# Two expert blocks computed during the first search, rows of x written during attention, the last scatter after the branch

## Chip, core and metric

The kernel runs on one core of a Trainium2 chip. The time is the device time of one execution in microseconds (us), the median of the runs. The engines are PE (matmul), DVE (vector), ACT (scalar), POOL (GpSimd) and SP (issues DMAs). Each takes its own instructions in order.

## What is computed

Two stages. First an RWKV-5 attention over r, k, v of shape (4 batches, 8 heads, 768 steps, 48), in which a state per head decays by w at every step. Then the result, as 3072 rows (tokens) of 384, goes through a mixture of 8 experts that is balanced by a global greedy rule:

```python
cap = N // E                                   # 384
logits = x @ w_gate                            # (3072, 8)
for idx in np.argsort(-logits.flatten()):      # best (token, expert) pair first
    tok, e = idx // E, idx % E
    if assigned[tok] >= 0 or counts[e] >= cap:
        continue
    assigned[tok] = e
    counts[e] += 1
for e in range(E):
    h = np.maximum(x[assigned == e] @ w1[e], 0.0)   # 384 -> 1024
    out[assigned == e] = h @ w2[e]                  # 1024 -> 384
```

So every expert gets exactly 384 tokens, which is three blocks of 128.

## The kernel before

**Attention** (class `Mild`). The sequence is cut into 6 chunks of 128 steps. A unit is one batch's chunk; there are N = 24 units, ordered chunk by chunk, so units 0 to 3 are chunk 0 of the four batches and units 20 to 23 are chunk 5. `Mild.run` writes the order of the instructions out by hand, one round for each unit n. A round works on several units at once: `turn(n+2)` transposes keys and queries on PE (kT_ps L456, rT_ps L462) which ACT and DVE move out, `diagonal(n+2)` is eight ACT operations (L484), `pairs(n+1)` is eight matmuls into g_ps (L494) and two masked copies on DVE (L496), `outputs(n)` is y_ps (L530) with `keep(n)` between its halves (kv_ps L509). After every fourth unit `gate` (lg_ps L557) and `logits` (lt_ps L567) put the gate's logits into the table LG, [128, 24, 8].

**Rows of x.** Attention's result is held transposed. `rows` transposes a unit back (four PE transposes, x_ps L579), ACT copies it (xr L581) and SP writes it to a table in DRAM, `x_rows` (L585), from which experts gather their tokens. Units 0 to 3 are done in the last two rounds, the others between the steps of the first search.

**The search** (class `Assignment`). The greedy rule is replaced by filling events: `likely` looks for the largest threshold at which some expert has at least 384 tokens that prefer it. Each of three rounds (`count`) compares all tokens with 16 candidates on DVE (ind), sums on PE (counts L882, L894) and picks a digit on DVE. That gives the expert (`fmax`), its tokens (`acc`), and their places (st_ps L998, L999). `tokens` makes a list of 384 token numbers (row, oh, vals on DVE, some_ps L1138, list_ps L1148). `leave` takes the tokens and the expert out of LG. Seven events are searched; the eighth expert takes what is left (`remainder`). A flag `ok` says whether every event was as the search supposes.

**The first search** stands between attention and the experts. Its steps are written out by hand too (`tc.manual_schedule`), with `rows` in the hooks `walk.between`, and with matmuls that nobody reads (`idle`, L412, 12 and 28 of them). The first expert's weights are loaded a quarter early, the rest behind the gather.

**Experts** (class `Experts`). For each: three gathers on POOL (xg L1222), weights of 3 MB on SP (L1218), nine transposes (xT_ps L1238), 24 matmuls of 384 columns into h_ps (L1247) with ReLU on ACT (L1248), and 24 into o_ps (L1254), eight for each block of 128 tokens, whose result ACT copies (o_sb L1256) and POOL scatters to the output (L1257). One matmul in float32 leaves two records in the trace, one transpose one record. Buffers are double: `turns[n % 2]`. `run` fetches expert n+1 while n is computed; here the scheduler puts the next search's instructions between the matmuls.

**The branch.** At the end every engine loads `ok` (L905) and branches (L1303) past an arm that computes everything again in a general way, in case the flag is 0.

Of the kernel before, what the change touches and what calls it, by code (L numbers as in the profile page):

```python
# [26 lines left out]
def attention_any(ctx, tc, r, k, v, w, u, wg, x_dram, LG, ident, walk):  # L27
# [181 lines left out]
    def outputs(n):  # L209
# [21 lines left out]
        nc.scalar.dma_start(x_dram[ts(b * C + c, 128), :], xt)  # L231
# [17 lines left out]
    def gate(n):  # L249
# [12 lines left out]
        nc.scalar.copy(LG[:, i, :], lg_ps)  # L262
# [12 lines left out]
class Mild:  # L275
# [243 lines left out]
    def outputs(self, n):  # L519
# [25 lines left out]
        xT = self.xpool.tile([128, HP, T], F32, name=f"x{n}")  # L545
# [18 lines left out]
    def logits(self, c):  # L564
        nc, B, lg = self.nc, self.B, self.lg
        lt_ps = self.walk.ps.tile([128, T], F32, name="lt_ps", tag="few")
        nc.tensor.transpose(lt_ps, lg, self.ident)  # L567
        nc.scalar.copy(self.LG.rearrange("p (b c) e -> p b c e", b=B)[:, :, c, :],
                       lt_ps.rearrange("p (b e) -> p b e", b=B)[:, :, 0:self.E])

    def rows(self, ns, tag):
# [3 lines left out]
        ps = self.ps.tile(shape, F32, name="x_ps", tag=tag)  # L575
        P = PD + D
        for i, n in enumerate(ns):
            for o in range(HP):
                nc.tensor.transpose(ps[:, i, o, 0:P], self.xts[n][0:P, o, :], self.ident[0:P, 0:P])  # L579
        xr = self.pool.tile([128, 2, H, D], F32, name="xr", bufs=4)  # L580
        nc.scalar.copy(xr[:, 0:m].rearrange("p i h d -> p (i h) d"),  # L581
                       ps.rearrange("p i o (z d) -> p (i o z) d", z=2)[:, :, 0:D])
        for i, n in enumerate(ns):
            b, c = self.units[n]
            nc.sync.dma_start(self.x_dram[ts(b * C + c, 128), :], xr[:, i].rearrange("p h d -> p (h d)"))  # L585
# [10 lines left out]
    def run(self):  # L596
# [21 lines left out]
        for n in range(N):  # L618
# [10 lines left out]
            else:  # L629
                if n + 3 < N:  # L630
                    self.again(n + 3)
                if n + 2 < N:
                    self.own_sum(n + 2)
                    self.turn(n + 2)
                    self.diagonal(n + 2)
                if n <= B:
                    self.keep(n - 1)
                if n + 1 < N:
                    self.pairs(n + 1)
            if n + 3 < N:  # L640
# [7 lines left out]
            if n == N - 2:  # L648
                walk.guess(walk.ps.tile([128, 128], F32, name="most_ps", tag="few"), self.ident)
            if n >= N - 2:  # L650
                self.rows((2 * (n - N + 2),), "kT_ps")
                self.rows((2 * (n - N + 2) + 1,), "rT_ps")
# [3 lines left out]
            if n == N - 3:  # L656
                walk.guess_most(self.LG.rearrange("p (b c) e -> p b c e", b=B)[:, :, 0:C - 1, :], AX.XYZ)
# [10 lines left out]
        self.rows((4, 5), "g_ps")  # L668
        self.left = [(n, n + 1) for n in range(6, N, 2)]
        self.turns = 1  # L670

    def some_rows(self, m):
        for _ in range(m):
            if self.left:
                self.rows(self.left.pop(0), ("g_ps", "y_ps")[self.turns % 2])
                self.turns += 1


class Assignment:
# [21 lines left out]
    def __init__(self, ctx, tc, ML, CAP):  # L701
        self.tc, self.nc, self.ML, self.CAP = tc, tc.nc, ML, CAP
# [40 lines left out]
        new("ok", [128, 1], I32)  # L743

        self.outs = ctx.enter_context(tc.tile_pool(name="s_outs", bufs=2))
# [4 lines left out]
    def constants(self):  # L750
# [86 lines left out]
        yield  # L837
        nc.gpsimd.memset(self.last, float(E * (E - 1) // 2))
# [33 lines left out]
    def count(self, pool, m, prop, cand, digit_of):  # L872
# [3 lines left out]
        ind = pool.tile([128, NT, ND], BF16, name="ind")  # L876
# [4 lines left out]
        for j in range(NT // G):  # L881
# [12 lines left out]
        nc.tensor.matmul(all_ps.rearrange("p d e -> p (d e)"), self.ones_h,  # L894
                         wide.rearrange("p d e -> p (d e)"), start=True, stop=True)
# [12 lines left out]
    def fill(self):  # L908
# [3 lines left out]
        tok = self.tokens(out["place"])  # L912
        self.leave(out["fmax"], out["acc"])
        return out["fmax"], tok

    def general_fill(self):
# [6 lines left out]
        self.leave(out["fmax"], out["acc"])  # L923
        return out["fmax"], tok

# [4 lines left out]
    def leave(self, fmax, acc):  # L930

        nc, pool, tt = self.nc, self.pool, self.tt
        NT, E = self.NT, self.E
        fe = pool.tile([128, E], F32, name="fe")
# [8 lines left out]
    def likely(self, fmax, acc, place, on_fmax=None):  # L943
# [11 lines left out]
        for g in range(3):  # L955
            all_ps = self.count(pool, m, prop, cand, self.digit_of)
            if g == 0:
                eq = pool.tile([128, NT, E], F32, name="eq")
# [36 lines left out]
        if on_fmax is not None:  # L995
# [3 lines left out]
        nc.tensor.matmul(st_ps[:, 1, :], self.rest_of, acc, start=True, stop=True)  # L999

# [8 lines left out]
        flag = pool.tile([128, 1], I32, name="flag")  # L1009
        nc.vector.scalar_tensor_tensor(out=flag, in0=upto[:, NT - 1:NT], scalar=float(CAP), in1=n_sole,  # L1010
                                       op0=ALU.is_equal, op1=ALU.mult)
        tt(self.ok, self.ok, flag, ALU.mult)
        tt(upto, upto, st_ps[:, 1, :], ALU.add)
        nc.vector.scalar_tensor_tensor(out=place, in0=upto, scalar=128.0, in1=acc, op0=ALU.add, op1=ALU.mult)

    def surely(self, pool, fmax, acc, place):
# [6 lines left out]
        eq = pool.tile([128, NT, E], F32, name="eq")  # L1023
# [64 lines left out]
    def remainder(self):  # L1088
# [12 lines left out]
        return fmax, self.tokens(place)  # L1101
# [19 lines left out]
    def tokens(self, place, tok=None):  # L1121

        nc, pool, ps, NT, tt, LO = self.nc, self.pool, self.ps, self.NT, self.tt, self.LO
        NC, Q = self.CAP // 128, 128 // LO
# [4 lines left out]
        row = pool.tile([128, NT, LO], F16, name="row")  # L1129
        tt(row, self.by_token(lo, LO), self.by_expert(self.iota[:, 0:LO]), ALU.is_equal)  # L1130
        oh = pool.tile([128, NT, NC * Q], F16, name="oh")
        tt(oh, self.by_token(hi, NC * Q), self.by_expert(self.hi_of), ALU.is_equal)
# [208 lines left out]
```

## Time and profile before

| | |
|---|---|
| median of 3 runs | 424.08 us (423.92 to 424.22) |
| profiled execution | 423.93 us, its span 422.2 us |
| busy share | PE 94%, PEld 63%, DVE 42%, ACT 36%, POOL 32% |
| chain that ended last | PE 70%, issue 13%, DVE 5%, POOL 4%, DMA 3% |
| groups | h_ps 133.5 us in 384 records, o_ps 127.5 us in 384 records |
| DMA | 54.09 MB, mean 128 GB/s |

The span runs from the first to the last instruction of the execution; what lies outside it is the difference to its own time. PE's busy time is modelled, so a PE that is always busy need not be at its peak. "issue" is time in which the engine waited for nothing that the profile shows. The stages in time: attention until about 122 us, the first search and the first gather until about 153 us, the experts until about 412 us, the end until 422.2 us.

### The profile page before, as it was taken

How to read it: one execution, taken by the hardware profiler on the slowest of the kernel's cores; microseconds unless marked ns; L12 is line 12 of the kernel's file. 1: busy time of each engine (PE TensorE's matmuls, PEld its weight loads, DVE VectorE, ACT ScalarE, POOL GpSimd, SP SyncE). 2: the span in 40 equal slices, each digit the busy share in tenths (PEclk: the TensorE clock that was granted, in tenths of full speed). 3: DMA queues.
4: the chain of work that ended last, by engine and by line, in shares of the span. 5: the costliest groups of instructions: out<-in, count | busy, mean ns of one | idle time of the engine just before them, and what ended most of it. 6: DMA issues, size and time to landing. Idle time of an engine off the chain costs nothing.

```text
span 422.2 us, 7769 instructions
## 1 busy us (share of the span) xinstructions
PE 398.0 (94%) x2960; PEld 266.6 (63%) x2960; DVE 177.7 (42%) x649; ACT 150.0 (36%) x383; POOL 134.2 (32%) x173
## 2 busy tenths in 40 slices
PE   5899999999987699999999999999999999999990
PEld 3788888788876555655655655555565565565550
DVE  5777886667548670057047038027207203000000
ACT  2788787778746121212212122022122112122100
POOL 5799887777200302101300310310310213010010
PEclk9999999999999899999999999999999999999997
DMA  7869976661039398105503601800910856010010
GB/s 152 167 123 186 197 139 134 118 131 20 3 113 334 98 313 302 39 19 183 193 37 123 251 37 55 321 37 6 348 39 19 321 221 210 17 39 19 0 40 22
DMA packets 94257, 54.09 MB, mean 128 GB/s; under 512 B 77185, under 2 KB 88834, under 8 KB 94210
## 3 DMA queue, kind: packets, MB, share of 16 engines
q1 hardware_dynamic: 90480, 44.05, 37.2%
q0 software_dynamic: 3072, 9.44, 6.3%
q8 instruction: 25, 0.41, 0.4%
q14 instruction: 22, 0.18, 0.1%
q10 hardware_dynamic: 658, 0.01, 0.1%
HBM read 44.06 MB, written 9.44 MB: 127 GB/s over the span
## 4 chain that ended last, share of the span: by engine, by line
PE 70%; issue 13%; DVE 5%; POOL 4%; DMA 3%; SPq 2%; ACT 0%; POOLq 0%; DVEq 0%; ACTq 0%
PE h_ps L1247 23%; PE o_ps L1254 22%; PE y_ps L530 7%; PE g_ps L494 5%; PE kv_ps L509 3%; PE kT_ps L456 2%; SPq L336 2%; PE rT_ps L462 2%; PE lg_ps L557 2%; PE xT_ps L1238 1%; POOL out_dram L1257 1%; DMA w<-in_moe_w_dram 1%; POOL xg L1222 1%; DMA vts<-in_v_dram 1%; POOL kss L431 1%
## 5 line engine op out<-in xcount | busy, mean ns | idle before, releaser
L1247 PE MATMUL h_ps<-xT,w 128*128 128x384 f32 x384 | 133.5, 497 | 0.9 <-ACT xT L1239 0.6
L1254 PE MATMUL o_ps<-w,hid 128*128 128x384 f32 x384 | 127.5, 486 | 0.0
L1254 PEld LDWEIGHTS o_ps<-w,hid 128*128 128x128 f32 x384 | 71.9, 190 | 47.2
L1247 PEld LDWEIGHTS h_ps<-xT,w 128*128 128x128 f32 x384 | 68.7, 190 | 41.6 <-issue 4.5
L1248 ACT ACTIVATE hid<-h_ps 128x384 f32<-128x384 f32 x64 | 31.4, 490 | 102.2 <-PE h_ps L1247 100.5
L484 ACT ACTIVATE AT<-ident,dd 128x128 f32<-128x128 f32 x192 | 58.7, 391 | 3.8 <-DVE dd L443 3.8
L1257 POOL DMA_INDIRECT out_dram<-o_sb,tok x21 | 20.7, 985 | 106.8 <-ACT o_sb L1256 81.0
L1222 POOL DMA_INDIRECT xg<-x_rows,tok x21 | 20.2, 964 | 99.4 <-PE h_ps L1247 62.7
L1256 ACT COPY o_sb<-o_ps 128x384 f32<-128x384 f32 x24 | 11.5, 478 | 108.4 <-PE o_ps L1254 100.2
L870 DVE TENSOR_TENSOR own<-counts,same 128x64 f32<-128x64 f32 x21 | 4.7, 223 | 99.7 <-PE counts L882 99.7
L496 DVE COPY_PREDICATED AT<-mask,g_ps 128x512 f32<-128x512 uint8 x48 | 32.7, 735 | 8.1 <-PE g_ps L494 6.9
L494 PE MATMUL g_ps<-rT,kT 48*128 48x128 f32 x384 | 27.9, 284 | 0.7 <-DVE AT L496 0.7
L431 POOL TENSOR_TENSOR kss<-krs,wk 128x384 f32<-128x384 f32 x24 | 24.2, 1013 | 6.2 <-DVE krs L340 5.0
L494 PEld LDWEIGHTS g_ps<-rT,kT 48*128 48x128 f32 x384 | 23.4, 187 | 4.4 <-issue 3.0
L530 PE MATMUL y_ps<-AT,vts 128*64 128x128 f32 x384 | 25.7, 276 | 0.0
L438 POOL TENSOR_TENSOR rk<-rk,u_bc 128x384 f32<-128x384 f32 x24 | 24.1, 1005 | 4.6 <-ACT u_bc L407 2.8
L437 POOL TENSOR_TENSOR rk<-krs 128x384 f32<-128x384 f32 x24 | 24.5, 1023 | 0.0
L530 PEld LDWEIGHTS y_ps<-AT,vts 128*64 128x64 f32 x384 | 20.6, 137 | 1.2 <-issue 0.7
L474 DVE TENSOR_TENSOR rT<-rT_ps,WR 112x512 f32<-112x512 f32 x23 | 15.8, 686 | 11.0 <-PE rT_ps L462 11.0
L546 ACT COPY x<-y_ps 128x512 f32<-128x512 f32 x24 | 14.0, 581 | 14.5 <-PE y_ps L530 14.5
L1239 ACT COPY xT<-xT_ps 128x384 f32<-128x384 f32 x24 | 10.8, 486 | 14.1 <-DVE cnt L890 10.9
L462 PE MATMUL rT_ps<-ident,krs 128*112 128x128 f32 x96 | 14.9, 279 | 0.0
(192 smaller groups left out, 401.1 us busy)
## 6 DMA issues: line engine op xcount, KB each, us to landing
w<-in_moe_w_dram SPq DMA_DIRECT2D x15, 1536.0 KB, 7.6
krs<-in_k_dram SPq DMA_DIRECT2D x24, 192.0 KB, 3.5
krs<-in_r_dram SPq DMA_DIRECT2D x24, 192.0 KB, 3.6
vts<-in_v_dram SPq DMA_DIRECT2D x24, 192.0 KB, 3.5
x_rows<-xr SPq DMA_DIRECT2D x24, 192.0 KB, 2.0
w<-in_moe_w_dram SPq DMA_DIRECT2D x1, 1152.0 KB, 5.6
w<-in_moe_w_dram SPq DMA_DIRECT2D x1, 384.0 KB, 3.1
xg<-x_rows,tok POOLq DMA_INDIRECT x21, 5.2
```

What stands on the lines that cost most here:

```text
L431: self.nc.gpsimd.tensor_mul(self.kss[:, n % self.NS].rearrange("p (g h) d -> p g h d", g=2)[:, :, :, 0:D], src, self.wk.rearrange("p (g h) ...
L437: nc.gpsimd.tensor_mul(rk, self.krs[:, n % self.NK, 1, 0:H, 0:D], self.krs[:, n % self.NK, 0, 0:H, 0:D])
L438: nc.gpsimd.tensor_mul(rk, rk, self.u_bc)
L484: nc.scalar.mul(AT[:, z, a, :], self.ident, dd[:, h:h + 1])
L494: nc.tensor.matmul(g_ps[:, z, a, :], kT[rows, a, :], rT[rows, a, :], start=True, stop=True)
L496: nc.vector.copy_predicated(out=AT[:, z], mask=self.mask.unsqueeze(1).to_broadcast([128, HP, T]), data=g_ps[:, z])
L530: nc.tensor.matmul(yv[q * PD:(q + 1) * PD, o // 2, o % 2, :], lhsT, rhs, start=(o // 2, q) not in seen, stop=stop, skip_group_check=True)
L1222: nc.gpsimd.indirect_dma_start(out=xg[:, c, :], out_offset=None, in_=x_dram, in_offset=bass.IndirectOffsetOnAxis(ap=tok[:, c:c + 1], axis=0))
L1247: nc.tensor.matmul(h_ps, w1[:, f, ts(j, 128)], xT[:, f, :], start=(f == 0), stop=(f == KD - 1))
L1248: nc.scalar.activation(hid[:, j, :], h_ps, AF.Relu)
L1254: nc.tensor.matmul(o_ps, hid[:, j, ts(c, 128)], w2[:, j, :], start=(j == 0), stop=(j == KF - 1))
L1257: nc.gpsimd.indirect_dma_start(out=to, out_offset=bass.IndirectOffsetOnAxis(ap=tok[:, c:c + 1], axis=0), in_=o_sb, in_offset=None)
```

## The change

1. **Early blocks.** `Assignment.early` is a new sequence of steps. From the tokens of the first 16 units it counts how many prefer each expert, and takes as `star` the one with the fewest, but at least `FEW` = 224. Of the first 20 units' tokens that prefer it, the first 256 are listed and gathered, taken out of LG, and counted as two blocks already given (`extra`, which `count` adds by one more matmul in each round). `Mild.run` places these steps in rounds 17 to 23 through the hook `step`. The weights of the star are loaded in round 18 and its tokens gathered in round 23. `Experts.early` computes the two blocks in 42 pieces, of which the hooks of the first search place some (`waits`) and `go(99)` the rest. The two fillers of `idle` are gone.
2. **The star is left to the end.** `book` and `choose` pass over the event in which the star fills and move each later one up, so that seven experts of three blocks come first and the star's one remaining block last. For this `later` searches one event ahead: its first turn runs two searches before it fetches. `hidden` computes m columns, 384 or 128.
3. **Rows of x** of units 0 to 19 are written in the rounds of attention, one unit a round, through a PSUM tile that is shared with the small matmuls ("few"); units 20 to 23 right after attention. The order of the rows in `x_rows` and of LG follows the units now, and `in_order` turns token numbers into output rows.
4. **First expert's weights** are loaded whole as soon as the expert is known.
5. **The last scatter**, of the star's block, is issued after the branch, from tiles (`o_last`, `tok_last`) that both arms write.

The core of the diff:

```diff
@@ Mild.run
+                step(n, "first")
                 if n + 3 < N:
                     self.again(n + 3)
                 if n + 2 < N:
                     self.own_sum(n + 2)
                     self.turn(n + 2)
+                if n <= N - B:
+                    self.rows((n - 1,), "few")
+                if n + 2 < N:
                     self.diagonal(n + 2)
+                step(n, "turned")
                 if n <= B:
                     self.keep(n - 1)
                 if n + 1 < N:
                     self.pairs(n + 1)
+                step(n, "paired")
...
-            if n >= N - 2:
-                self.rows((2 * (n - N + 2),), "kT_ps")
-                self.rows((2 * (n - N + 2) + 1,), "rT_ps")
...
@@ Assignment.count
+        for i, x in enumerate((extra, wide)[extra is None:]):
+            nc.tensor.matmul(all_ps.rearrange("p d e -> p (d e)"), self.ones_h,
+                             x.rearrange("p d e -> p (d e)"), start=(i == 0), stop=(x is wide))
...
@@ Assignment.early, cut to its steps (A: the first 16 units, Z: the next 4)
+        prop = prefer(A, KA)                      # DVE
+        yield
+        nc.tensor.matmul(cnt_ps.rearrange("p i e -> p (i e)"), self.ones, prop.rearrange("p i e -> p (i e)"),
+                         start=True, stop=True)
+        named(prop, A, KA)                        # DVE
+        yield
...
+        on_star(self.star)                        # SP: the star's weights
+        yield
+        chosen(A)                                 # DVE
+        st_ps = sums(A, KA)                       # PE, two matmuls
+        yield
+        lo, hi = places(st_ps, A, KA)             # DVE
+        yield
+        row = row_of(lo, KA)                      # DVE
+        vals = values(hi, A, KA)
+        yield
+        some_ps = listed(row, vals, KA)           # PE, four matmuls
+        parts(some_ps, 0)                         # DVE
+        yield
+        prop = prefer(Z, B)                       # DVE
+        named(prop, Z, B)
+        chosen(Z)
+        yield
+        st_ps = sums(Z, B)                        # PE
+        lo, hi = places(st_ps, Z, B)              # DVE
+        row = row_of(lo, B)
+        vals = values(hi, Z, B)
+        yield
+        some_ps = listed(row, vals, B)            # PE
+        parts(some_ps, 1)                         # DVE
...
+        yield
+        self.numbers(both, NE, tok)               # PE and DVE
+        on_tokens(tok)                            # POOL: two gathers
+        yield
...
...
@@ the first search
-                walk.between = lambda step: mild.some_rows(1 if step == "each" else 2)
...
-                mild.idle(12, "kT_ps")
...
-                mild.idle(28, "kT_ps")
...
+            steps = [(U - 7, "first"), (U - 7, "paired"), (U - 6, "turned"), (U - 6, "paired"), (U - 5, "turned"),
+                     (U - 5, "paired"), (U - 4, "turned"), (U - 3, "first"), (U - 3, "turned"), (U - 2, "paired"),
+                     (U - 1, "first"), (U - 1, "paired"), (U - 1, "last")]
...
+                mild.rows((U - 4, U - 3), "g_ps")
+                waits = iter([0, 3, 2, 4, 2, 5, 6, 1])
...
+                walk.likely(**first, on_fmax=lambda fmax: have.update(v=x.load_weights(1, fmax)))
+                tok = walk.tokens(first["place"])
+                walk.between = lambda kind: None
+                xg = x.gather(1, tok)
+                go(99)
...
+        def later():
+            was = walk.event()
+            walk.book(was)
+            walk.leave(was)
+            for n in range(2, E):
+                rest = n == E - 1
+                now = walk.remainder() if rest else walk.event()
+                walk.book(now, surely=rest)
+                walk.choose(was, now)
+                yield x.fetch(n, was["fmax"], walk.tokens(was["place"]))
+                if not rest:
+                    walk.leave(now)
+                was = now
+            yield x.fetch(E, walk.star, walk.tokens(walk.star_place, 1))
...
+    x.scatter(o_last, tok_last, out_rows[NT - 1])
```

Between the counts and `on_star` stand seven small DVE operations, from `cnt` to the star's number; the last steps, in round 23, take the tokens out of LG and set `extra`. In `waits` a number is that of pieces placed at a hook, and 0 stands for the rows of units 22 and 23. The hooks come in the order each, all (three times), then behind the sums of `likely`, then behind some_ps of `tokens`. A piece is a block's three transposes, one matmul of `e_h_ps` (256 columns) or one of `e_o_ps` (384 columns).

## Prediction

> **What bounds the kernel now.** I read the busy times by stage first, then one attention round and the gap in order of time, then the chain of waits, the DMA issues and the last lines' sequencer events.
>
> Busy time by stage (us, then busy time and count of each engine, then granted clock, DMA share, GB/s):
>
> ```profile
> 75.00:107.00 32.00, 32.00 (x558) 27.16 (x558) 21.63 (x47) 25.93 (x76) 25.74 (x30) 1.00 0.45 89
> ...
> 122.00:153.00 31.00, 23.34 (x177) 18.51 (x177) 21.52 (x105) 10.78 (x17) 3.37 (x5) 0.94 0.63 212
> ...
> 182.00:215.00 33.00, 33.00 (x127) 19.25 (x126) 12.76 (x61) 6.17 (x14) 5.92 (x6) 1.00 0.37 132
> ```
>
> PE (first figure) fills attention and the expert stage. Only in the gap between them, while the first search runs on DVE, is it idle: 31.0 - 23.3 = 7.7 us.
>
> In order of time: one round of attention, rows of x, and the fillers:
>
> ```profile
> 101.45 0.60 PE L462 MATMUL rT_ps<-ident,krs 128*112 128x128 f32 x4
> ...
> 101.98 1.16 PE L494 MATMUL g_ps<-rT,kT 48*128 48x128 f32 x16
> ...
> 103.07 0.67 PE L530 MATMUL y_ps<-rT,states 48*64 48x128 f32 x16
> ...
> 103.26 1.36 DVE L496 COPY_PREDICATED AT<-mask,g_ps 128x512 f32<-128x512 uint8 x2 [0.48 <-PE g_ps L494]
> ...
> 115.22 0.93 PE L579 MATMUL x_ps<-ident,x 112*128 112x112 f32 x8
> ...
> 134.41 1.51 PE L412 MATMUL unread_ps<-ident 128*128 128x128 f32 x12
> ...
> 140.24 4.83 PE L412 MATMUL unread_ps<-ident 128*128 128x128 f32 x28
> ```
>
> A round is 4.19 us of back-to-back PE (kT_ps starts at 100.97 and again at 105.16). The fillers' 6.3 us is work that nobody reads, so the gap holds 7.7 + 6.3 = 14.0 us that useful work could take. That is all this change can win on PE.
>
> The chain that ended last (start, us, what):
>
> ```profile
> 147.03 5.56 DMA w<-in_moe_w_dram
> 152.73 0.88 PE h_ps L1247 x2
> ...
> 165.07 10.32 PE o_ps L1254 x32
> ...
> 198.49 10.32 PE o_ps L1254 x32
> ```
>
> DMA issues (us to landing last):
>
> ```profile
> xg<-x_rows,tok POOLq DMA_INDIRECT x21, 5.2
> ...
> xg<-x_rows,tok_first POOLq DMA_INDIRECT x3, 3.0
> ```
>
> An expert takes 198.49 - 165.07 = 33.42 us, and one record of 384 columns 10.32/32 = 0.3225 us. A gather lands in 3.0 us alone, 5.2 us beside weights.
>
> Sequencer events of the branch and of the end:
>
> ```profile
> L1303 ACTq COMPARE_BRANCH  x1: 50/50/50, 412.6 to 412.6; - x1
> ...
> L1303 ACTq EVENT_SEMAPHORE  x1: 17/17/17, 415.1 to 415.1; - x1
> ...
> L1303 POOLq INC_SWDGE_SEM  x1: 1148/1148/1148, 416.2 to 416.2; - x1
> ...
> L1336 POOLq DRAIN  x3: 40/107/3995, 417.4 to 421.9; - x3
> ```
>
> A taken branch costs ACT 2.5 us; POOL's end (jump, semaphores, a 4.0 us drain) runs after the last scatter.
>
> **The change, part by part** (against the profiled execution: 423.93 us, span 422.2 us, so 1.73 us outside; the median, 424.08, is 0.15 higher).
>
> *Data.* From the reference's inputs, the expert chosen is number 1 (230 of the first 16 units' tokens prefer it, the fewest above 224; 294 of 20 units), it fills last, and all 256 early tokens end there. So the fallback arm does not run.
>
> *Expert stage.* Per expert, PE does 48 records of h_ps and 48 of o_ps (31.2 us by rows L1247 and L1254 at about 0.325) and 9 transposes of xT (1.0): 32.2. One expert becomes one block: 48 records of 128 columns (at 0.107, as 16 x_ps in 1.72 us) 5.2, 16 of o_ps 5.2, three transposes 0.3: 10.7, so -21.5. New: one more count matmul in each of 18 rounds at 0.07 (+1.3), a token list more (+0.4), a round of search that used to precede the stage (+0.4). Sum -19.4. The DVE work of `book` and `choose`, about 12 small operations a search at 0.07 to 0.2, is hidden by seven matmults of h_ps (4.6 us against 4.1 us of DVE before); uncovered, it costs up to 1 us an expert.
>
> *Rows of x in attention.* 20 units; 4 records cost 0.93/2 = 0.46 on a full PE. Rounds 5 to 20: 16 x 0.46 = +7.4. Rounds 1 to 4 partly wait for POOL (4.0 us a round): +1.2. Leaving rounds 22 and 23: -1.9. The extra ACT copy (0.43) fits (ACT 25.9 of 32). On SP each write of rows waits for its copy with the next loads queued behind it, some 2 us; those loads are used two rounds later: nothing. If PE had hidden slack the rows would be free, if dependencies add up, 0.6 each: -7.4 to +2.5.
>
> *Choosing in attention.* About 11 small matmuls: +1.1. PE is in order, and some wait. (a) Unit 18: the sums follow g_ps but need `chosen`, which stands on DVE behind two mask copies (1.36) and the seven operations of the star: 2.1 us, with y_ps of unit 18 queued behind. (b) Unit 20: the list needs the PSUM tile that ACT still copies rows from: 0.6. (c) Unit 21: sums wait for LG of units 16 to 19 and five dependent DVE steps: 0.5. (d) g_ps of unit 23 waits for the mask copies that slipped behind `places` and `values`: 1.0. (e) list_ps of unit 23: 0.3. Together 4.5; bounds 1 and 8. With gate bookkeeping of 0.7, attention ends 7.4 + 1.2 - 1.9 + 1.1 + 4.5 + 0.7 = +13.0 later. Star weights (3 MB) go into a time with DMA share 0.0 to 0.25: hidden.
>
> *The gap.* Two blocks are new on PE: 6 transposes at 0.11 (0.7), 48 records of 256 columns at two thirds of 0.3225 (10.3), 32 records of o_ps (10.3): 21.3 us, against 14.0 us of idle time and fillers and 16 of the 20 rows' worth of transposes (7.4) that left. Before: last LG at 123.06, steady h_ps from 152.73 less the twelve records already done (3.9) = 148.8, so 25.7 us. After: the search's chain on DVE still sets the pace while PE puts pieces beneath it. From LG to the first counts 1.3, as before; first round 3.7 (3.5 before; the first e_h must wait for two ACT copies of xT); second 3.2 (four matmults of e_h, 1.72, beneath 2.2 us of DVE between a count and the next); third to the sums of acc 3.5; then places, row, oh and vals 2.9 with six matmults (2.6) beneath, list 1.0: list_ps at +15.6. Before it was +17.1, since DVE also did `leave` and the next search's first steps there. Of the 42 pieces 23 are done by then. Left are 3 of e_h (0.43 each) and 16 of e_o (0.645): 11.6. Then counts 0.4, nine transposes 1.0, and the waits for `wide` and for the last copy of xT 1.2: 2.6. In all 29.8 us, +4.1; bounds +2.5 (no bubbles) and +6. The next expert's gather (tok at +16.2, landing 6.5 later) and weights (issued at about +14, landing 9 later) lie beneath the 11.6; without that cover they would cost what the 152.73 above shows, some 4 us.
>
> *Second expert.* The first turn of `later` runs two searches before it fetches. In PE's order the list falls behind 24 h_ps and 17 o_ps, S + 15.8 + 11.0 + searches 2.5 = S + 29.3 (S: start of h_ps). Gathers start at S + 30.7, 1.27 apart, behind a scatter on POOL; the second lands at S + 32.0 + 4.6 = S + 36.6, but PE arrives at S + 32.5: +4.1. Bounds: 0 (landing 3.0 and earlier DVE) and 6.
>
> After that wait the clock may be halved: before, PE nearly idle from 136.0 to 139.2 was followed by clock 0.50 until 143.5. Once more that costs 1.7; I take 0.8. The Trainium skill (TensorE: Matmul & The Clock Gate, Part 1) has free-running windows of 3.4 us, of which a 4.1 us pause holds a whole one in about one phase in five; by that estimate the term would be 0.3 and the time half a microsecond less.
>
> *Last scatter.* Before: from ACT's copy end (412.5) to the end 9.7 us. After: POOL has jumped earlier, but the scatter waits for ACT's semaphore past its own branch: 2.6, start 0.3, then landing 2.6 and end 0.8, or issue 1.0, drain and end. The drain is 0.1 to 4.0: total 6.3 to 8.7; I take 7.7: -2.0. The Trainium skill (Advanced Engine Details and Errata, Control Flow Timing) gives about 108 ns for a compare-and-branch; ACT's row is 2.5 us to the next event and decides. By the page the gain would be 2.4 us larger.
>
> Sum: 13.0 + 4.1 - 19.4 + 4.1 + 0.8 - 2.0 = +0.6, and 0.5 for search waits that reappear in seven experts: +1.1. 422.2 + 1.1 + 1.73 + 0.15 = 425.2 us.
>
> **Rivals.** *PE has slack in attention.* PE's ends are modelled, and if the rounds are set by a chain of handovers the 16 rows cost nothing: 425.2 - 7.4 = 417.8. For: early rounds wait for POOL. Against: DVE waits for rT_ps in nearly every round. It decides below 0.34 us a round: then the kernel is faster. *The second fetch is in time*: no wait and no halved clock, 425.2 - 4.9 = 420.3. Against: the order on PE. *Every search is late*: `book` and `choose` outlast seven matmults in six searches, 1 us each: 431. For: only 0.5 us of cover. *The choice fails* and the arm runs everything again: over 800. Against: the inputs.
>
> **How the numbers follow.** Forecast 0.53 (own range 422 to 429), slack 0.24, in time 0.06, late searches 0.16, fallback 0.01. A measurement tells 0.2% (0.85 us). Faster: 0.24 + 0.06 + 0.04 of the forecast's low end = 0.34; same: 0.12 of the forecast; slower: 0.37 + 0.16 + 0.01 = 0.54. The range runs from just under the slack case, 417, to just past the late searches, 432.
>
> **What would show it.** Right: x_ps in rounds of 4.65 us; last LG near 136; a PE wait before e_st_ps of 2 us; steady h_ps near 166; an xT_ps wait of 4 us once; ends of o_ps near 415; ACT's event 2.6 us after its copy. Wrong: rounds still 4.2 us, xT_ps without a wait, or gaps before some_ps in every expert.

## The result, and the profile after

The changed kernel takes 435.27 us (median of 4 runs, 435.02 to 436.10); the kernel before took 424.15 us (423.92 to 424.33) beside it. The ratio is 1.0266, with an interval of 1.0248 to 1.0284: 11.1 us slower, where +1.1 was forecast. The profiled execution took 435.47 us with a span of 433.65 us, 11.44 us longer than the span before.

Busy time by stage of the changed kernel, in the columns shown for the kernel before (attention, the gap with the first search, one expert):

```profile
75.00:107.00 32.00, 30.41 (x527) 25.93 (x525) 21.99 (x56) 24.84 (x71) 21.05 (x26) 1.00 0.84 157
142.00:173.00 31.00, 27.98 (x144) 19.81 (x145) 19.47 (x89) 8.23 (x21) 4.84 (x5) 1.00 0.44 159
216.00:249.00 33.00, 33.00 (x127) 19.28 (x126) 13.56 (x72) 6.35 (x14) 5.22 (x6) 1.00 0.38 132
```

The gap is now filled: PE is busy for 28.0 of 31.0 us, most of it work on the two early blocks. What went up is the time before the gap, and the first expert behind it. Five points of each profile give the stages; all times are starts, in us. Attention runs from kT to the last LG, the gap from there to the first h_ps, the experts from there to the last copy of o_ps, the tail from there to the end. "kT" is the first kT_ps out of kss, which moves by up to 1.4 us between these profiles, so attention is counted from there. (e1 to e12 are the experiments below. The first h_ps of the kernel before, 148.8, is the reckoned start that the prediction explains; for e1 and e2, which have the same gap, it isn't given.)

| kernel | kT | last LG | first h_ps | last copy of o_ps | span | attention | gap | experts | tail |
|---|---|---|---|---|---|---|---|---|---|
| before | 20.48 | 122.85 | 148.8 | 412.02 | 422.21 | 102.37 | 25.95 | 263.2 | 10.19 |
| changed | 20.59 | 142.61 | 172.88 | 424.54 | 433.65 | 122.02 | 30.27 | 251.66 | 9.11 |
| e1 | 20.71 | 123.09 | - | 412.66 | 421.75 | 102.38 | - | - | 9.09 |
| e2 | 20.67 | 130.77 | - | 420.06 | 430.40 | 110.10 | - | - | 10.34 |
| e3 | 21.24 | 137.02 | 167.30 | 419.17 | 428.37 | 115.78 | 30.28 | 251.87 | 9.20 |
| e4 | 21.78 | 139.24 | 169.51 | 421.06 | 430.27 | 117.46 | 30.27 | 251.55 | 9.21 |
| e5 | 21.88 | 135.45 | 165.71 | 417.21 | 426.43 | 113.57 | 30.26 | 251.50 | 9.22 |
| e6 | 20.91 | 141.46 | 171.72 | 416.94 | 426.33 | 120.55 | 30.26 | 245.22 | 9.39 |
| e7 | 21.41 | 142.54 | 175.25 | 418.86 | 428.14 | 121.13 | 32.71 | 243.61 | 9.28 |
| e8 | 21.01 | 134.58 | 167.28 | 410.88 | 420.37 | 113.57 | 32.70 | 243.60 | 9.49 |
| e9 | 21.82 | 142.86 | 173.12 | 424.46 | 433.64 | 121.04 | 30.26 | 251.34 | 9.18 |
| e10 | 20.77 | 142.90 | 173.16 | 424.92 | 435.10 | 122.13 | 30.26 | 251.76 | 10.18 |
| e11 | 20.85 | 140.35 | 170.61 | 422.15 | 431.38 | 119.50 | 30.26 | 251.54 | 9.23 |
| e12 | 20.76 | 134.03 | 166.75 | 410.35 | 419.69 | 113.27 | 32.72 | 243.60 | 9.34 |

Changed against before: attention +19.65, gap +4.3, experts -11.5, tail -1.1. The forecast had +13.0, +4.1, -14.0 (-19.4 + 4.1 + 0.8 + 0.5) and -2.0. So the gap is as reckoned, attention is 6.7 us worse, the experts 2.5 and the tail 0.9.

In order of time on PE, the stretch of attention in which the star is chosen (start, us, what, how long PE was idle before it, and who ended that):

```profile
106.98 0.58 PE L578 MATMUL x_ps<-ident,x 112*128 112x112 f32 x4 [1.07 <-DVE e_cnt L1147]
...
110.85 0.20 PE L1091 MATMUL e_st_ps<-e_acc,ones 128*128 128x16 bf16 x1 [2.19 <-DVE e_acc L1087]
...
112.95 1.94 PE L530 MATMUL y_ps<-AT,vts 128*64 128x128 f32 x16
...
117.76 0.58 PE L578 MATMUL x_ps<-ident,x 112*128 112x112 f32 x4 [1.17 <-DVE e_after L871]
```

The 2.19 us is wait (a) of the prediction (2.1). The waits of x_ps, 1.07 and 1.17 us, were not in it: the rows of x are transposed into the one PSUM tile that the choosing's matmuls use too, so they wait until DVE has read e_cnt_ps and e_st_ps. And y_ps of unit 18, 1.06 us in other rounds, takes 1.94. The same stretch cut where the granted clock changes, and the first expert's pause beside it (columns as above, PE's busy time first, the clock third from the end):

```profile
106.03:109.44 3.41, 1.67 (x20) 1.37 (x20) 3.20 (x9) 1.97 (x7) 2.90 (x3) 1.00 0.45 96
109.44:112.85 3.41, 2.00 (x34) 1.66 (x34) 1.35 (x3) 0.98 (x4) 0.00 (x0) 0.50 0.39 97
112.85:116.27 3.42, 3.42 (x29) 3.09 (x28) 0.94 (x3) 0.84 (x2) 2.56 (x4) 0.50 1.00 398
...
205.01:208.43 3.42, 0.66 (x3) 0.04 (x1) 0.00 (x0) 0.00 (x0) 1.92 (x2) 1.00 1.06 393
208.43:211.84 3.41, 2.23 (x8) 1.58 (x9) 0.00 (x0) 0.93 (x2) 0.00 (x0) 0.50 0.44 162
```

PE was busy for 1.67 of 3.41 us, and the clock was 0.50 for the next 6.83 us. In these 6.83 us PE was busy for 5.4, work of 2.7 at full clock: 2.7 us lost, by no wait at all.

The second expert's fetch is as it was predicted, to a tenth (chain of waits: start, us, what). S is 172.88, so the list was due at S + 29.3 = 202.2:

```profile
202.33 0.05 PE list_ps L1357
...
203.75 5.81 DMA xg<-x_rows,tok
209.56 0.04 issue
209.61 1.75 PE xT_ps L1457 x6
```

PE stood ready at 205.67 and waited for 3.94 us (predicted 4.1), and the clock was 0.50 from 208.43 to 215.25.

The end, as sequencer events of the branch (L1604) and of the last line:

```profile
L1604 ACTq COMPARE_BRANCH  x1: 50/50/50, 425.1 to 425.1; - x1
L1604 ACTq EVENT_SEMAPHORE  x1: 17/17/17, 427.5 to 427.5; - x1
...
L1640 POOLq DRAIN  x3: 40/112/5208, 427.6 to 433.4; - x3
```

ACT's event comes 2.5 us after its copy ended (425.02), POOL issues the scatter at 427.82, and a drain of 5.2 us, which now holds the scatter's landing, runs to the end: 1.1 us gained in all.

### The profile page after: what moved, and what is told of

The parts are those of the page before. It is cut to its first block, busy times and chain, and to the rows that moved or that the text cites. A ratio compares the mean times of both kernels' runs of the same rounds, so it can differ in the third digit from the quotient of the medians.

```text
span 433.6 us, 8028 instructions
## 1 busy us (share of the span) xinstructions
PE 401.8 (93%) x3002; PEld 272.1 (63%) x3002; DVE 200.6 (46%) x795; ACT 153.6 (35%) x401; POOL 134.3 (31%) x172
## 4 chain that ended last, share of the span: by engine, by line
PE 68%; DMA 13%; DVE 7%; issue 6%; ACT 2%; another core or an unknown queue 1%; POOL 1%; POOLq 0%; ACTq 0%; DVEq 0%
PE h_ps L1466 20%; PE o_ps L1478 18%; DMA out_dram<-o_sb,to 11%; PE y_ps L530 7%; PE g_ps L494 5%; PE kv_ps L509 3%; PE e_o_ps L1521 2%; PE kT_ps L456 2%; PE rT_ps L462 2%; PE x_ps L578 2%; PE xT_ps L1457 2%; PE e_h_ps L1513 1%; DVE AT L496 1%; PE lg_ps L557 1%; DMA xg<-x_rows,tok 1%
## 5 line engine op out<-in xcount | busy, mean ns | idle before, releaser
L1466 PE MATMUL h_ps<-xT,w 128*128 128x384 f32 (+1 forms) x384 | 124.2, 472 | 0.6 <-ACT xT L1458 0.6
L1478 PE MATMUL o_ps<-w,hid 128*128 128x384 f32 x352 | 119.6, 492 | 0.0
L1478 PEld LDWEIGHTS o_ps<-w,hid 128*128 128x128 f32 x352 | 65.5, 192 | 41.7 <-issue 1.4
L1466 PEld LDWEIGHTS h_ps<-xT,w 128*128 128x128 f32 x384 | 64.6, 191 | 36.1 <-issue 7.2
L1468 ACT ACTIVATE hid<-h_ps 128x384 f32<-128x384 f32 (+1 forms) x64 | 29.7, 464 | 94.2 <-PE h_ps L1466 87.3
L1472 POOL DMA_INDIRECT out_dram<-o_sb,to x21 | 20.8, 988 | 129.0 <-ACT o_sb L1484 95.2
L1442 POOL DMA_INDIRECT xg<-x_rows,tok x22 | 21.2, 965 | 95.8 <-issue 60.6
L1484 ACT COPY o_sb<-o_ps 128x384 f32<-128x384 f32 x21 | 10.1, 479 | 92.9 <-PE o_ps L1478 84.2
L530 PE MATMUL y_ps<-AT,vts 128*64 128x128 f32 x384 | 26.6, 282 | 0.0
L546 ACT COPY x<-y_ps 128x512 f32<-128x512 f32 x24 | 14.0, 585 | 22.1 <-PE y_ps L530 18.6
L578 PE MATMUL x_ps<-ident,x 112*128 112x112 f32 x96 | 13.0, 261 | 3.5 <-ACT x L546 1.2
```

The source lines that it names most:

```text
L530: nc.tensor.matmul(yv[q * PD:(q + 1) * PD, o // 2, o % 2, :], lhsT, rhs, start=(o // 2, q) not in seen, stop=stop, skip_group_check=True)
L1466: nc.tensor.matmul(h_ps[:, 0:m], w1[:, f, ts(j, 128)], xT[:, f, 0:m], start=(f == 0), stop=(f == KD - 1))
L1468: nc.scalar.activation(hid[:, j, 0:m], h_ps[:, 0:m], AF.Relu)
L1478: nc.tensor.matmul(o_ps, hid[:, j, ts(c, 128)], w2[:, j, :], start=(j == 0), stop=(j == KF - 1))
```

## The experiments

All times are medians beside runs of the kernel before on the same chip, where that took 424.43 to 424.52 us. The changed kernel's 1.0266 would be about 435.8 us there, and it measured 435.86 (e9).

**e1: the last scatter alone.** On the kernel before:

```diff
-x.run((xg, tok, w1, w2), walk.fill, out_rows)
+x.run((xg, tok, w1, w2), walk.fill, [*out_rows[0:NT - 1], None])
...
+    nc.gpsimd.indirect_dma_start(out=out_rows[NT - 1], out_offset=bass.IndirectOffsetOnAxis(ap=tok_last, axis=0),
+                                 in_=o_last, in_offset=None)
```

> The kernel before with one part of the change: the last scatter is issued behind the branch. Theory (a shorter tail): from the end of the last o_ps copy to the end of the span took 9.2 us before and 8.6 us in the changed kernel, counted from the copy's start 9.7 and 9.1; so this kernel should gain 0.5 to 1.1 us: 423.0 to 423.6. The forecast's own term said -2.0, which would be 422.1. Rival (the drain only moves, and ACT's branch, 2.4 us to its event, stands in its place): 424.1, no difference.

Measured: 423.46 us against 424.50, ratio 0.9978 (0.9967 to 0.9988). The tail shrank from 10.19 to 9.09 us. (The expectation misquotes the tail before: it was 9.7 us from the copy's end and 10.2 from its start; the gain of 1.1 is right.) The theory holds, and the prediction's -2.0 was too much.

**e2: the rows of x alone.** On the kernel before, rows of units 0 to 19 in the rounds; nothing is chosen early:

```diff
                     self.turn(n + 2)
+                if n <= N - B:
+                    self.rows((n - 1,), "few")
+                if n + 2 < N:
                     self.diagonal(n + 2)
...
```

> The kernel before with one part of the change: the rows of x of units 0 to 19 are transposed and written in attention's rounds, nothing is chosen early. Theory (PE is full in attention and the gap's length is set by DVE): rounds of 4.58 us as in the changed kernel, attention longer by 8.1 less 1.9 for the four rows that leave rounds 22 and 23, the gap unchanged: +6.2, 430.3. Rival one (rows beneath the search held its matmuls up): the gap gets shorter by some 1 us: 429.3. Rival two (PE has slack in the rounds, which the choosing alone used up): rounds of 4.2 us, 424.

Measured: 432.12 us, ratio 1.0181 (1.0167 to 1.0194), +7.6. Rounds, by the starts of kT_ps in this run:

```profile
104.47 0.65 PE L456 MATMUL kT_ps<-ident,kss 128*112 128x128 f32 x4
...
109.05 0.65 PE L456 MATMUL kT_ps<-ident,kss 128*112 128x128 f32 x4
```

They take 4.58 us (before 4.19): four transposes cost 0.39 on a full PE, against 0.46 reckoned. Attention grew by 7.73 us (forecast 7.4 + 1.2 - 1.9 = 6.7; this run's expectation said 6.2). By the starts of g_ps, counted from kT, the rows had cost 2.5 us after the fourth of them (g_ps of unit 5 at 15.80, before 13.32) and 8.7 us after the twentieth (unit 21 at 94.36, before 85.70). The four rows that leave rounds 22 and 23 then give back 0.9 us and not 1.9, because y_ps of unit 23 now waits for ACT's copy of the unit ahead, where rows stood before:

```profile
126.56 0.67 PE L530 MATMUL y_ps<-rT,states 48*64 48x128 f32 x16 [0.69 <-ACT x L546]
```

The second rival, PE with slack in its rounds, is out, and so is the first: from the last LG to the last copy took 289.29 us here and 289.17 before. The gap did not change although the clock was 0.50 for 13.65 us of it. In these 13.65 us DVE was busy for 11.56 and PE for 6.95: DVE's chain sets the gap's pace there.

**e3: the sums one step later on PE.** On the changed kernel:

```diff
         chosen(A)
+        yield
         st_ps = sums(A, KA)
...
-            steps = [(U - 7, "first"), (U - 7, "paired"), (U - 6, "turned"), (U - 6, "paired"), (U - 5, "turned"),
+            steps = [(U - 7, "first"), (U - 7, "paired"), (U - 6, "turned"), (U - 6, "paired"), (U - 5, "first"), (U - 5, "turned"),
```

> The changed kernel with one edit: the matmuls of the sums (e_st_ps of units 0 to 15) stand one step later on PE, behind y_ps of unit 18 in place of ahead of it. Theory (PE waits in order, and this wait of 2.19 us brings the clock down to 0.5 from 111 to 116, which costs some 2.7 us more): both go, 435.3 - 4.9 = 430.4, with clock 1.0 throughout units 18 and 19. Rival one (DVE is what is full there: star, masks and places): the wait returns at the next g_ps, 435. Rival two (the halving belongs to another cause than this wait): only 2.2 us go, 433.1, and the clock is still 0.5 near 112.

Measured: 429.29 us, ratio 1.0107 (1.0093 to 1.0121), 6.5 less than the changed kernel. The sums now find e_acc ready, and the stretches behind are at full clock (timeline, then the time by stretch):

```profile
111.49 0.18 PE L1091 MATMUL e_st_ps<-e_acc,ones 128*128 128x16 bf16 x1
```

```profile
110.42:113.83 3.41, 2.13 (x31) 1.68 (x28) 2.95 (x10) 1.82 (x5) 2.06 (x3) 1.00 0.53 115
113.83:117.24 3.41, 3.41 (x66) 2.98 (x68) 3.12 (x6) 2.82 (x9) 1.39 (x2) 1.00 1.01 406
```

Two matmuls of 0.2 us, moved by one step, take their wait and the halved clock with them: the theory holds, both rivals fall. The other runs agree: in all seven profiles with the sums in their old place (the changed kernel twice, e4, e6, e7, e10, e11) the clock fell to 0.50 near them, and in none of the four with later sums (e3, e5, e8, e12). The stretch from 110.42 has PE busy for 0.62 of its time and is not followed by half clock. The median fell by 1.6 us more than the theory's 4.9; that is the size of the late copy of y_ps (e9), which is absent here.

**e4: another PSUM tile for three rows.**

```diff
...
-                    self.rows((n - 1,), "few")
+                    self.rows((n - 1,), "counts" if n >= N - 6 else "few")
```

> The changed kernel with one edit: the rows of x of units 17 to 19 are transposed into the PSUM tile of kv_ps in place of the one that the choosing's matmuls use. Their waits for DVE's readers of e_cnt_ps (1.07 us) and e_st_ps (1.17 us), and the list's for ACT's copy (0.57), should be gone. Theory (the waits lie in a row, and the sums still wait for the star on DVE): the first is given back at e_st_ps, the other two are gained: -1.7, 433.6, and clock 0.5 stays. Rival (each wait counts by itself): -2.8, 432.5.

Measured: 432.10 us, ratio 1.0174 (1.0161 to 1.0188), 3.7 less. The first wait came back at the sums, as the theory said:

```profile
112.02 0.17 PE L1091 MATMUL e_st_ps<-e_acc,ones 128*128 128x16 bf16 x1 [3.44 <-DVE e_acc L1087]
```

3.44 is 2.19 + 1.07 and a little; the waits of 1.17 and 0.57 are gone. The sum is larger than either number for two reasons outside it: the clock was 0.50 for 3.41 us and not 6.83, and the late copy of y_ps is absent.

**e5: all waits of the choosing.** e3 and e4 together, with the second choice's sums, list and numbers later too:

```diff
-                     (U - 5, "paired"), (U - 4, "turned"), (U - 3, "first"), (U - 3, "turned"), (U - 2, "paired"),
-                     (U - 1, "first"), (U - 1, "paired"), (U - 1, "last")]
+                     (U - 5, "paired"), (U - 4, "turned"), (U - 3, "first"), (U - 3, "paired"), (U - 2, "last"),
+                     (U - 1, "turned"), (U - 1, "paired"), (U - 1, "last")]
```

> The changed kernel with all waits of the choosing in attention taken away: the sums one step later (as in e3), rows of units 17 to 19 in the tile of kv_ps (as in e4), and the second choice's sums, list and token numbers one or two steps later on PE. Theory (in-order waits and what they draw after them): e3's -6.5, and 1.07 + 1.17 + 0.57 + 0.81 + 0.85 of the other waits of PE: -11.0 against the changed kernel, about 424.8 on a chip where the kernel before takes 424.5; what is left of the excess in attention is the rows' 8 us and about 1 of matmuls. Rival (DVE fills up in units 18 to 22, and the waits come back at g_ps and rT): no more than -8, 428.

Measured: 427.92 us, ratio 1.0073 (1.0052 to 1.0095), -7.9. This miss is on the rival's side. Two of the waits that remain:

```profile
112.15 0.17 PE L1091 MATMUL e_st_ps<-e_acc,ones 128*128 128x16 bf16 x1 [1.39 <-DVE e_acc L1087]
...
118.77 0.58 PE L578 MATMUL x_ps<-ident,x 112*128 112x112 f32 x4 [0.92 <-DVE krs L340]
```

With the earlier waits gone PE reaches the sums sooner, and DVE, with the star and two mask copies (1.33 us) ahead of e_acc, is not done. With 0.35 and 0.73 later on, 3.4 us of waits for DVE remain, about what attention still lacks against e2 (113.57 to 110.10).

**e6: no look-ahead.** Each search of later() is followed by its list and fetch; choose() is left out:

```diff
-            was = walk.event()
-            walk.book(was)
-            walk.leave(was)
             for n in range(2, E):
...
+                was = walk.event()
+                walk.book(was)
                 yield x.fetch(n, was["fmax"], walk.tokens(was["place"]))
...
+                walk.leave(was)
+            walk.book(walk.remainder(), surely=True)
```

> The changed kernel without its look-ahead in later(): each expert's search is followed at once by its list and its fetch, and choose() is left out, so that the case of a star that fills before the others is not handled (with these inputs it fills last). Theory (two searches ahead of the second fetch make PE wait 3.94 us for the gather, and the clock of 0.5 for the 6.83 us behind it costs 2.8): both go, 435.8 - 6.7 = 429.1. Rival one (the gather lands late anyway because the weights are loaded beside it): the wait stays, at half or more, 432 to 434. Rival two (the halving has no link to the wait): -3.9, 431.9.

Measured: 428.10 us, ratio 1.0117 (1.0079 to 1.0156), -7.8; experts 245.22 against 251.66, -6.44. In the chain of waits the list stands 14.55 us behind the first h_ps, and xT_ps follows o_ps without a pause:

```profile
186.27 0.01 PE list_ps L1357
...
188.96 10.32 PE o_ps L1478 x32
199.28 0.66 PE xT_ps L1457 x6
```

The clock stays at 1.0 through this stage. The wait of 3.94 is gone, and 2.5 more: the theory holds. For the halved clock it had 2.8, which is also what the busy times give: PE was busy for 2.23 + 3.41 us at half clock, work of 2.8 us at full clock. The rest of the median's 7.8 is attention, 120.55 us against 122.02: the late copy of y_ps is absent here too.

**e7: the second search in the gap.**

```diff
-                go(99)
+                walk.leave(first)
+                walk.book(first, first=True)
+                go(7)
+                more = iter([1, 3, 1, 3, 1, 3, 99])
+                walk.between = lambda kind: go(next(more))
+                second = walk.event()
+                walk.between = lambda kind: None
                 to = walk.in_order(tok)
-                walk.book(first, first=True)
-                walk.leave(first)
                 walk.bound(ident)
...
-            was = walk.event()
+            was = second
```

> The changed kernel with the second search moved from the first expert's turn to the gap, where the last 19 pieces of the early blocks leave DVE idle: leave and book first, then the search, whose pauses are filled with pieces (7 ahead of it, then 1 and 3 by turns). Theory: the list of the second expert stands a search (about 11 us) earlier on PE, its gather lands in time, and the wait of 3.94 us and the halved clock go (-6.7); in the gap the search needs some 13 us against the 11.6 us of pieces: +1 to +2. Sum -5: 430.8. Rival (the pieces held up by the search's handovers cost as much as the wait): 435.

Measured: 428.89 us, ratio 1.0105 (1.0085 to 1.0125), -7.0. The gap grew by 2.44 us, the experts fell by 8.05. The list of the second expert stands 18.6 us behind the first h_ps, the gather is in time. The gap pays for three rounds of count matmuls that the expert no longer does. Together that is -5.6, against -5 expected. Attention, 121.13 us against 122.02, is not this edit's: the late copy of y_ps is absent, half clock near the sums lasts 3.41 us and not 6.83, and a stretch of half clock from 25.72 to 29.13 costs some of that again.

**e8: e5 and e7 together.**

> e5 and e7 together. Theory (two separate losses): -11.0 and -5: 419.8, 1.1% under the kernel before. Rival (they are not separate: an attention that ends earlier only lets the search wait elsewhere): above 423.

Measured: 422.05 us (6 runs, 421.83 to 423.00) against 424.52, ratio 0.9945 (0.9928 to 0.9962): faster than both kernels, though by 2.5 us and not 4.7, and 1.0 us of that the last scatter gives alone (e1). Attention is e5's (113.57), the rest e7's (32.70 and 243.60): two separate losses. The 2.3 us missing against the expectation are less than the 3.1 that e5 missed.

**e9: the changed kernel again.**

> The changed kernel once more, unchanged, for two questions. One: ACT's last copy of y_ps began 1.67 us after y_ps had ended, with no releaser in the trace. If that belongs to the program, it is there again at the same copy; if it belonged to that one execution, it is gone and the time of this run's profile is some 1.5 us shorter. Two: the stretches at half clock. If they follow from PE's idle time on the program's own course, they come again from about 109 and 208 us; if their place varies from one execution to the next, their number and length do too. Time: 435.3 to 436.

Measured: 435.86 us, ratio 1.0273 (1.0251 to 1.0294). ACT's copy is late again (timeline of ACT, this run, then e6, whose code up to there is the same):

```profile
140.38 0.59 ACT L546 COPY x<-y_ps 128x512 f32<-128x512 f32 x1 [3.39 <-remote]
```

```profile
138.99 0.59 ACT L546 COPY x<-y_ps 128x512 f32<-128x512 f32 x1 [1.80 <-PE y_ps L530]
```

So it seems to belong to the program: both profiles of the changed kernel, e10 and e11 show it (1.6 to 1.7 us behind the end of y_ps), e12 shows one of 1.16 us, and in e3 to e8 the copy follows within 0.06 us. "remote" says that the view names no releaser. The semaphore events kept in the traces show more: in the changed kernel's first profile the PE semaphore for which the copy waits rose at 140.11, 1.65 us behind the modelled end of y_ps (138.46), and the copy began 0.02 us later; in e6 it rose 0.04 us behind that end. So it was not ACT that was late but PE's signal, or y_ps itself, whose end is modelled. Why stays open. The half clock came after the same two waits, but for 3.41 us each time (from 112.04 and 211.03) in place of 6.83; attention is 1.0 us shorter for it. The experts are shorter by only 0.3 us, since PE waited longer for the second gather (4.04 and 0.57 us in place of 3.94).

**e10: the last scatter put back.**

```diff
-x.run((1, xg, to, *have["v"]), later(), (a for a in [*out_rows[2:NT - 1], None]))
+x.run((1, xg, to, *have["v"]), later(), iter(out_rows[2:NT]))
...
-    x.scatter(o_last, tok_last, out_rows[NT - 1])
```

> The changed kernel with the last scatter issued in its old place, ahead of the branch. Theory (what e1 gained is lost again): the span behind the last copy of o_ps grows from 9.1 to 10.2 us, +1.0: 436.3 to 436.8. Rival (the shorter tail of before came from its own surroundings): no difference.

Measured: 438.11 us (435.80 to 439.79), ratio 1.0327 (1.0295 to 1.0359), 2.2 above e9. The tail is 10.2 us, +1.1, as the theory has it. The other 1.1 us of the medians is not assigned: the two profiled executions differ by 1.5 us in all, and the two intervals all but touch.

**e11: the rows two units behind.**

```diff
-                if n <= N - B:
-                    self.rows((n - 1,), "few")
+                if 2 <= n <= N - B + 1:
+                    self.rows((n - 2,), "few")
```

> The changed kernel with the rows of x taken two units behind in each round in place of one. Theory (the first rounds with rows pay for a wait that the sum had not: x_ps waits 1.23 us for ACT's copy of the unit just done): -1.2, and the distance from the second to the third kT_ps of kss falls from 5.57 to some 4.4 us; no other round changes. Rival (POOL sets the early rounds, at 4.0 us): no difference.

Measured: 433.11 us, ratio 1.0226 (1.0200 to 1.0252), -2.7 against e9. The round of the first row in the changed kernel, and the same round and the first row in this one:

```profile
20.59 0.65 PE L456 MATMUL kT_ps<-ident,kss 128*112 128x128 f32 x4
22.90 0.61 PE L578 MATMUL x_ps<-ident,x 112*128 112x112 f32 x4 [1.23 <-ACT x L546]
26.16 0.65 PE L456 MATMUL kT_ps<-ident,kss 128*112 128x128 f32 x4
```

```profile
20.85 0.65 PE L456 MATMUL kT_ps<-ident,kss 128*112 128x128 f32 x4
24.85 0.65 PE L456 MATMUL kT_ps<-ident,kss 128*112 128x128 f32 x4 [0.19 <-POOL kss L431]
...
25.77 0.55 PE L578 MATMUL x_ps<-ident,x 112*128 112x112 f32 x4
```

5.57 us became 4.00, but that round has no row here. The first row stands one round later, waits for nothing, and its round takes 4.12 us (the next kT_ps starts at 28.97), against 3.99 in the kernel before. So the wait is gone and has not moved; the row itself costs 0.1 us there. Attention is 1.5 us shorter than in e9; the rest of the median's 2.7 is not assigned.

**e12: e8 with sums still later, and rows two behind.**

> e8 (422.05, against 424.52 for the kernel before) with the sums another half round later (e5 still shows 1.39 us of wait for e_acc there), the list of units 0 to 15 behind g_ps of unit 21, and the rows of x two units behind. Theory (in-order waits): -1.4, -0.9 and -1.2: 418.6, 1.4% under the kernel before. Rival (DVE is full in units 18 to 21 and hands its lateness on): above 420.5.

Measured: 422.22 us (9 runs, 421.26 to 423.82), ratio 0.9958 (0.9940 to 0.9977): no better than e8. Two things meet. With its rows e12 is 1.6 us ahead of e8 early on (ACT's copy of y_ps of unit 14, counted from kT, at 67.46 against 69.04), and 1.4 us in unit 22 (107.05 against 108.45): so the sums and the list gained nothing, and for them the rival holds. In unit 23 another 1.1 us is lost to the late copy of y_ps (1.16 us here, none in e8; see e9). DVE hands its lateness on to the next matmul that shares the PSUM tile:

```profile
117.93 1.08 PE L557 MATMUL lg_ps<-x,wgp 128*32 128x128 f32 x32 [1.72 <-DVE e_some L871]
```

## Why the prediction was wrong

Its mechanism, a gain in the expert stage that attention and the gap pay back, is what happened. The balance, +0.6 and 0.5, fell on the wrong sizes; the time lies 3.3 us above its range. Step by step:

- **Data, star weights, search beneath h_ps: right.** One block of the star came last, the load of its weights ended no wait of PE, and no expert shows a gap before some_ps. The rival of late searches is out: the period is 33.74 us, 0.32 longer.
- **Rows: the rounds right in sum, by luck; the return mis-sized.** Rounds 1 to 4 cost 2.5 us and not 1.2, most of it in the round of the first row, 1.6 us, where x_ps waits for ACT (e11 takes that away); rounds 5 to 20 cost 16 x 0.39 = 6.2 and not 7.4. Together that is 8.7 for 8.6. But the rows that leave rounds 22 and 23 gave back 0.9 and not 1.9 (e2): 7.7 against 6.7.
- **Choosing: this step failed.** Forecast 1.1 + 4.5 + 0.7 = 6.3; measured 122.02 - 110.10 = 11.9. The five waits named came as they were sized: (a) 2.19 for 2.1, (b) 0.57 for 0.6, (c) 0.81 for 0.5, (d) 0.85 for 1.0, (e) 0.28 for 0.3, together 4.7 for 4.5. Three things were not in the sum. First, 1.07 and 1.17 us in which x_ps waits for DVE's readers of e_cnt_ps and e_st_ps: the prediction followed the shared PSUM tile from a row to the list (b), but not from the choosing's matmuls to the next row. Second, the halved clock, 2.7 us: it was charged for the gather's wait alone, and not for the waits in attention. Third, the late last copy of y_ps, 1.6 us (from the start of unit 23's y_ps to the last LG 5.84 us, in e6 4.22), which no run explains. Against that the small matmuls and bookkeeping cost 0.7 by what is left, not 1.8. 4.7 + 2.2 + 2.7 + 1.6 + 0.7 = 11.9.
- **Gap: right.** 30.27 us for 29.8.
- **Second expert: wait right (3.94 for 4.1), what follows it mis-sized.** The halved clock took 2.5 us (e6: 6.44 - 3.94; 2.8 by the busy times), not 0.8. The estimate from a page, 0.3, was further off. The Trainium skill (TensorE: Matmul & The Clock Gate, Part 1) gives an idle window of 3413 ns as what lowers the clock; the stretch ahead of the halving had PE busy for 0.66 of 3.42 us, so no wholly idle window was needed.
- **Expert stage without that: -18.0 (251.66 - 6.44 - 263.2) for -18.9.** The period of an expert is 0.32 us longer, more than the 0.2 of the added count matmuls; the rest is not assigned.
- **Last scatter: -1.1 for -2.0** (e1, e10). ACT's branch took 2.5 us as the row said, and the drain behind, with the landing in it, came out at 5.2 us, where the sum had allowed 0.1 to 4.0.

The terms' errors are 1.0 (rows), 5.6 (choosing), 0.2, 1.7 (halved clock), 0.9, 0.9 and -0.2 (the gather's wait): 10.1 of the 10.3 us missed. The slack rival (0.24) is refuted by e2's rounds, the rival of the fetch in time by the 3.94 us. The range held bounds of 1 to 8 us for the waits, but none for a halved clock in attention, so its upper end had no case with all of them.

## What to carry to other kernels

A matmul put into a full in-order stream has two dependences to price: its operands, and the last reader of the PSUM tile it is given, and the next user of that tile pays as well. A wait of 2 us on PE should be priced with the clock behind it: here 2.19 us cost their own length and, by an estimate from the busy times at half clock, 1.7 to 2.7 us more (3.41 or 6.83 us at 0.50), and moving two 0.2 us matmuls by a step took both away (e3). In the gap, where DVE sets the pace, 13.65 us of half clock cost nothing (e2). Before moving work to a busy stage, look for another engine's idle time elsewhere: the second search fitted into the gap, where the last pieces leave DVE idle, for 2.4 us more gap and 8.1 us less in the experts (e7). Neither that nor the shorter waits in attention (e5) brought the kernel under the one before; the two together did (e8).

## What the runs showed of the hardware that was not expected

- **The clock moves in steps of 3.41 us.** In all profiles the clock held for whole multiples of that between two changes (at half clock 3.41, 6.83 or 13.65 us). Cut into that grid, and counted from the 100th us to where the last matmuls end, 17 stretches at full clock had PE busy for 0.09 to 0.49 of their time, and each was followed by half clock; with 0.50 or more (one in e9 has 0.50) none was. The limit is not sharp, and the busy share alone does not decide: in e7 a stretch from 22.30 us with 0.64 was followed by half clock, and of the stretches that hold the last matmul one with 0.41 was (e4) and one with 0.43 was not (e5). At half clock, stretches busy for 0.77 or less were followed by another, those of 0.97 or more by full clock; between them one of 0.88 stayed at half, and two of 0.86 and 0.89 came back. The free-running window of 3413 ns in the Trainium skill (TensorE: Matmul & The Clock Gate, Part 1) agrees with the length; the condition of an idle window does not, since a stretch busy for 0.49 was low enough (the changed kernel, 106.03 to 109.44).
- **Two executions of one program differ by it.** The changed kernel had 6.83 us of half clock in attention in one profile and 3.41 in the other (e9), 1.0 us of difference at the last LG.
- **ACT's copy of y_ps of unit 23 started 1.6 to 1.7 us behind that matmul's modelled end** in four profiles of three programs (the changed kernel twice, e10, e11) and 1.16 us behind it in e12, but at most 0.06 us in e3 to e8. The PE semaphore it waits for rose late; what sets that was not found.
